# Attention before two expert layers on Trainium2: small products of 8 values a token, and of two inverse scales, made by POOL instead of VectorE

## The chip, the cores and the metric

The kernel runs on one core of one Trainium2 chip. A core has five engines, each of which runs its own instructions in order: TensorE (PE: matmuls, and transposes made by matmul), VectorE (DVE), ScalarE (ACT), GpSimd (POOL) and SyncE (SP, here the issuer of most DMAs). Engines wait for one another by semaphores. The metric is the time of one execution in microseconds on the device.

## The reference, cut to what matters

```
kv  = einsum('bhsd,bhse->bhde', k, v)             # 8 batches, 8 heads, 576 x 64
out = einsum('bhsd,bhde->bhse', q, kv)
out = out / sqrt(mean(out*out, -1) + 1e-6) * g_norm   # per token and head
x   = out as 4608 tokens x 512
h   = x @ w_in                                    # 512 x 2048
g   = max(h, 0) + alpha * min(h, 0)
y   = g @ w_out                                   # 2048 x 512
logits = y @ w_gate; e = argmax(logits)           # 8 experts, one per token
out = softmax(logits)[e] * sigmoid(y @ w_output_gate)[e] * (max(y @ w1[e], 0) @ w2[e])
```

For each token the norm needs 8 values, one per head: the sum of squares over 64 elements, its mean plus 1e-6, and that to the power -0.5. These 128x8 tiles (128 tokens, 8 heads) are what the change is about.

## The kernel before, in words

**Tiling.** 4608 tokens are 36 tiles of 128; three tiles make a block (12 blocks, i = 0 to 11). Products in 32 bits are made of three f16 matmuls: each operand is scaled by a power of two and split into a high and a low half ("hi", "lo"). For the scaling, pow2 (lines 108 to 121, three VectorE operations) turns a maximum into a scale and its inverse.

**Attention for block i** is att_steps(i), a list of steps that is fed between other work. For each tile, tr scales and splits q: qam is the maximum per head (line 273, VectorE), pow2 gives qsc and its inverse qiv, qiv is multiplied by the inverse scale kvi of kv (line 278 on 128 rows; for the ninth tile of a pair of batches line 282 does it on two halves of 64 rows), qs = q * qsc is made by POOL (line 284), split by ScalarE (287) and VectorE (288), and transposed by a DMA (290). Then om: matmuls into ops (line 311), ScalarE squares ops into xs (316), VectorE reduces xs to st, 128x8 (318), multiplies st twice by qiv (321), makes ms (323), and POOL raises ms to -0.5 into rs (325). Beside it VectorE takes the maximum of st over the heads, qm (328), and makes the power-of-two scale xinv of it (329 to 337). rs is multiplied by qm and qiv (340), ops by rs into xs (343); ScalarE and POOL split xs into x (347, 348), and a DMA transposes x into the block's tile (351). Blocks 0 and 1 take another way for q ("split_q" is false there), with no products by qiv.

**The first expert layer for block i.** 16 pieces h (h_piece, line 586, 12 matmuls each, two PSUM buffers): ScalarE makes m (589), VectorE r (591), ScalarE the hi half of g (593), VectorE its lo half (594; POOL in blocks 0 and 1). m and r have two buffers each. Then y (605), its maximum (655), the split into row (663 on ScalarE, 664 on VectorE), a DMA transpose to yT (668) and the logits l (678).

**Routing.** From the logits come the one-hot oh (up to 704), the rank matmuls rk (712 to 716), the positions pos (718 to 725), and three scatters by POOL (728), indirect DMAs that write the tokens' numbers into one list; each waits until the one before has landed. The rows are stored by SP (757, after 751).

**Order.** The program's text gives the steps in an order of interleaving, and a scheduler with a simulated timeline then sets the order on each engine, PE, ACT, DVE, POOL and SP alike; so a few changed instructions move others around them. In the last block and the second expert layer the order is set by hand.

Of the kernel before, what the change touches and what calls it, by code (L numbers as in the profile page):

```python
# [9 lines left out]
F32 = mybir.dt.float32  # L10
# [4 lines left out]
ALU = mybir.AluOpType  # L15
# [4 lines left out]
P = 128  # L20
B, H, S, D = 8, 8, 576, 64
# [29 lines left out]
EPS = 1e-6  # L51
# [6 lines left out]
def body(ctx: ExitStack, tc, q, k, v, g_norm, w_in, w_out, alpha, w_gate, w_og, w1, w2, out):  # L58
    nc = tc.nc
    pe, dve, act, pool, sp = nc.tensor, nc.vector, nc.scalar, nc.gpsimd, nc.sync  # L60
# [45 lines left out]
    def pow2(am, nm, out_s, out_inv, top=14, wide=False):  # L106


        e = small.tile([P, am.shape[1]], I32, tag="pw_e", name="pw_e" + nm, padded_shape=[P, E])
        dve.tensor_scalar(out=e, in0=am.bitcast(I32), scalar1=0x7FF00000 if wide else 0x7F800000, scalar2=None,  # L110
                          op0=ALU.bitwise_and)
        if wide:
            dve.tensor_scalar(out=e, in0=e, scalar1=float((896 + top + 1) << 20), scalar2=float((896 + 254) << 20),
                              op0=ALU.max, op1=ALU.min)
            dve.tensor_scalar(out=out_inv.bitcast(I32), in0=e, scalar1=8.0, scalar2=float(-((896 + top) << 23)),
                              op0=ALU.mult, op1=ALU.add)
        else:
            dve.tensor_scalar(out=out_inv.bitcast(I32), in0=e, scalar1=float((top + 1) << 23),
                              scalar2=float(-(top << 23)), op0=ALU.max, op1=ALU.add)
        dve.tensor_scalar(out=out_s.bitcast(I32), in0=out_inv.bitcast(I32), scalar1=-1.0, scalar2=float(254 << 23),  # L120
                          op0=ALU.mult, op1=ALU.add)
# [47 lines left out]
    kvp, qp, at = right("kvp", 2), right("qp", 2), right("at", 2)  # L169
# [74 lines left out]
    kv16, kvi = {}, {}  # L244
# [16 lines left out]
    def att_steps(i):  # L261
        G, t0 = divmod(i * TB, 9)
        ts = [t0 + u for u in range(TB)]
        qT, qi_ = {}, {}
        split_q = i >= SPLIT_Q

        def tr(t):
            nm = f"_{G}_{t}"
            n = 5 * G + t // 2
            qv = q_in[n][:, :, t % 2 if t < 8 else 0, :]  # L270
            if split_q:
                am = small.tile([P, H], F32, tag="am8", name="qam" + nm)
                dve.tensor_reduce(out=am, in_=qv, axis=AX.X, op=ALU.max, apply_absolute_value=True)
                s_ = small.tile([P, H], F32, tag="qsc", name="qsc" + nm)
                iv = qi_[t] = small.tile([P, H], F32, tag="qiv", name="qiv" + nm, bufs=4)
                pow2(am, "q" + nm, s_, iv)
                if t < 8:
                    dve.tensor_tensor(out=iv, in0=iv, in1=kvi[2 * G + t // 4], op=ALU.mult)
                else:
                    for half in range(2):  # L280
                        sl = slice(64 * half, 64 * half + 64)
                        dve.tensor_tensor(out=iv[sl], in0=iv[sl], in1=kvi[2 * G + half][sl], op=ALU.mult)
                qs = at.tile([P, H, D], F32, tag="xs", name="qs" + nm, bufs=3)
                pool.tensor_tensor(out=qs, in0=qv, in1=s_.unsqueeze(2).to_broadcast([P, H, D]), op=ALU.mult)
                qs = qs.rearrange("p a b -> p (a b)")
                q16 = at.tile([P, 2, DM], F16, tag="x16", name="q16" + nm)
                act.copy(out=q16[:, 0, :], in_=qs)
                dve.tensor_tensor(out=q16[:, 1, :], in0=qs, in1=q16[:, 0, :], op=ALU.subtract)
                qT[t] = at.tile([P, 2 * NC, P], F16, tag="qT", name="qT" + nm)
                sp.dma_start_transpose(out=qT[t], in_=q16.rearrange("p a b -> p (a b)"))  # L290
            else:
                qj = scratch[(1, 2, 0, 3, 4, 5)[t]]
                act.copy(out=qj.rearrange("p (h d) -> p h d", h=H), in_=qv)
                qps = ps_a.tile([P, NPAIR, P], F32, tag="a", name="qps" + nm)
                for hp in range(NPAIR):
                    pe.transpose(qps[:, hp, :], qj[:, hp * P:(hp + 1) * P], ident)
                qT[t] = at.tile([P, NPAIR, P], F32, tag="qT", name="qT" + nm)
                act.copy(out=qT[t], in_=qps)
            if t % 2 == 1 or t == 8:
                load_q(n + 2)  # L300

        def om(t):
            nm = f"_{G}_{t}"
# [11 lines left out]
            xs = at.tile([P, DM], F32, tag="xs", name="xs" + nm, bufs=3)  # L315
            act.activation(out=xs, in_=ops.rearrange("p a b -> p (a b)"), func=AF.Square)
            st = small.tile([P, H], F32, tag="st", name="st" + nm)
            dve.tensor_reduce(out=st, in_=xs.rearrange("p (h d) -> p h d", h=H), axis=AX.X, op=ALU.add)
            if split_q:
                for _ in range(2):  # L320
                    dve.tensor_tensor(out=st, in0=st, in1=qi_[t], op=ALU.mult)
            ms = small.tile([P, H], F32, tag="ms", name="ms" + nm)
            dve.tensor_scalar(out=ms, in0=st, scalar1=1.0 / D, scalar2=EPS, op0=ALU.mult, op1=ALU.add)
            rs = small.tile([P, H], F32, tag="rs", name="rs" + nm)
            pool.tensor_tensor(out=rs, in0=ms, in1=mhalf, op=ALU.pow)  # L325

# [880 lines left out]
```

## Time and profile before

| | us |
|---|---|
| median of 3 runs | 1522.31 |
| the 3 runs | 1513.83, 1522.31, 1522.7 |
| profiled execution, its own time | 1527.29 |
| its span, first to last instruction | 1525.5 |
| busy: PE | 1338.3 (88%) |
| busy: VectorE | 870.1 (57%) |
| busy: ScalarE | 580.7 (38%) |
| busy: POOL | 397.7 (26%) |

The profile is of one execution. Busy shares are means over the span, and the stages have different limits: to about 222 us weights and kv are prepared, 222 to 288 us is the end of the second block, then follow the steady blocks, and past some 1000 us the experts of the second layer, where VectorE and POOL have little to do. The time in front of an instruction in which its engine was idle is printed in brackets with what ended it. PEclk is TensorE's granted clock, in shares of full speed.

### The profile page before, as it was taken

The numbers are of one execution on the slowest core, as the hardware profiler recorded it, in microseconds if no ns is written. First come the engines' busy times: TensorE is split into PE (matmuls) and PEld (weight loads), VectorE is DVE, ScalarE is ACT, GpSimd is POOL, SyncE is SP. The second block draws the span as 40 slices with busy tenths as digits, with TensorE's granted clock in tenths as the row PEclk, the third lists the DMA queues.
The fourth block names the chain that finished last, engine by engine and source line by source line (L and its number), as shares of the span: only waits on it lengthen the run. The fifth ranks groups of instructions, "written<-read, shape, count | busy, mean of one in ns | idle before, by whom it ended". The sixth has DMA issues, their size and how long they took to land.

```text
span 1525.5 us, 22316 instructions
## 1 busy us (share of the span) xinstructions
PE 1338.3 (88%) x7586; PEld 680.4 (45%) x7586; DVE 870.1 (57%) x2406; ACT 580.7 (38%) x959; POOL 397.7 (26%) x383
## 2 busy tenths in 40 slices
PE   4687775698899898999999999998789978998998
PEld 3443332354445454555554555543333433443443
DVE  6888788675779696969696877535112112121221
ACT  3455535344556454655454655411111111111111
POOL 3455545232122232212121212011311111221211
PEclk9689888899999999999999999999899999999999
DMA  9732116646677677766745765147886986679665
GB/s 273 189 94 86 61 50 150 127 77 172 174 193 190 186 181 162 213 175 160 206 109 136 183 159 134 22 146 137 229 262 146 216 244 161 131 184 237 119 151 152
DMA packets 344835, 243.25 MB, mean 159 GB/s; under 512 B 267388, under 2 KB 300172, under 8 KB 342160
## 3 DMA queue, kind: packets, MB, share of 16 engines
q1 hardware_dynamic: 327792, 206.11, 55.3%
q0 software_dynamic: 7712, 18.92, 4.1%
q10 hardware_dynamic: 9216, 16.78, 3.3%
q8 instruction: 60, 0.98, 0.3%
q14 instruction: 55, 0.45, 0.1%
HBM read 244.66 MB, written 53.97 MB: 196 GB/s over the span
## 4 chain that ended last, share of the span: by engine, by line
PE 26%; DVE 19%; DMA 17%; issue 16%; SPq 14%; ACT 4%; POOL 3%; POOLq 0%; ACTq 0%; DVEq 0%
PE h L586 10%; PE y L605 6%; SPq L986 4%; PE bh_d L977 4%; PE bo_d L998 3%; DMA rawe<-in_moe_w_dram 3%; DMA yT<-row 3%; SPq L864 2%; DVE r L591 2%; SPq L949 2%; DMA out_dram<-ob_d,idx_d 2%; DMA hT_d<-h_d 2%; DMA ws<-wlo_w 2%; DVE wlo_w L387 1%; SPq L952 1%
## 5 line engine op out<-in xcount | busy, mean ns | idle before, releaser
L586 PE MATMUL h<-x,wi 128*128 128x384 f16 x2304 | 416.8, 333 | 28.0 <-ACT m L589 19.6
L605 PE MATMUL y<-wo,g 128*128 128x512 f16 x1728 | 416.4, 389 | 27.8 <-ACT wo L455 6.7
L586 PEld LDWEIGHTS <-wi 128*128 128x128 f16 x2304 | 224.4, 100 | 188.5 <-issue 38.5
L605 PEld LDWEIGHTS <-g 128*128 128x128 f16 x1728 | 167.4, 100 | 221.7 <-issue 40.6
L983 DVE CAST h_d<-br_d 128x512 f16<-128x512 f32 x74 | 32.3, 436 | 355.8 <-DMA hT_d<-h_d 314.1
L998 PE MATMUL bo_d<-lane,hT_d 128*128 128x512 f16 x888 | 206.3, 391 | 26.5 <-DMA hT_d<-h_d 26.5
L977 PE MATMUL bh_d<-lane,byT_d 128*128 128x512 f16 x888 | 202.2, 385 | 15.9 <-DMA byT_d<-yg 8.3
L998 PEld LDWEIGHTS <-hT_d 128*128 128x128 f16 x888 | 88.6, 100 | 139.3 <-DMA hT_d<-h_d 28.9
L593 ACT CAST g<-r 128x384 f16<-128x384 f32 x192 | 97.4, 509 | 133.4 <-DVE r L591 131.2
L591 DVE SCALAR_TENSOR_TENSOR r<-m,alphat 128x384 f32<-128x384 f32 x192 | 126.9, 662 | 30.1 <-ACT m L589 28.7
L977 PEld LDWEIGHTS <-byT_d 128*128 128x128 f16 x888 | 87.8, 99 | 124.6 <-DMA byT_d<-yg 8.8
L981 ACT ACTIVATE br_d<-bh_d 128x512 f32<-128x512 f32 x74 | 44.2, 597 | 208.3 <-PE bh_d L977 113.7
L325 POOL TENSOR_TENSOR rs<-ms,mhalf 128x8 f32<-128x8 f32 x36 | 67.0, 1864 | 173.9 <-DVE qm L328 158.3
L728 POOL DMA_INDIRECT lst<-ids,pos x36 | 39.2, 1090 | 271.4 <-DMA lst<-ids,pos 108.7
L594 DVE TENSOR_TENSOR g<-r,g 128x384 f16<-128x384 f32 x160 | 92.5, 579 | 24.2 <-ACT g L593 23.5
L589 ACT ACTIVATE m<-h,scal 128x384 f32<-128x384 f32 x160 | 91.5, 574 | 37.8 <-PE h L586 36.5
L387 DVE SCALAR_TENSOR_TENSOR wlo_w<-rawe,es_w,whi_w 128x1024 f16<-128x1024 f32 x64 | 87.1, 1376 | 27.1 <-ACT whi_w L386 10.7
L386 ACT ACTIVATE whi_w<-rawe,es_w 128x1024 f16<-128x1024 f32 x64 | 71.2, 1142 | 56.8 <-DMA ws<-whi_w 35.6
L856 POOL DMA_INDIRECT yg<-ytab,idx_d x37 | 38.2, 1032 | 188.1 <-issue 125.3
L1001 ACT ACTIVATE ob_d<-bo_d,msc_d 128x512 f32<-128x512 f32 x37 | 25.4, 687 | 162.3 <-PE bo_d L998 157.7
L526 ACT ACTIVATE eab_w<-rawe 128x1024 bf16<-128x1024 f32 x64 | 66.9, 1055 | 47.7 <-DMA rawe<-in_moe_w_dram 43.2
L1002 POOL DMA_INDIRECT out_dram<-ob_d,idx_d x37 | 39.0, 1055 | 165.4 <-ACT ob_d L1001 143.0
(304 smaller groups left out, 1395.8 us busy)
## 6 DMA issues: line engine op xcount, KB each, us to landing
lane<-ws SPq DMA_DIRECT2D x74, 2048.0 KB
rawe<-in_moe_w_dram SPq DMA_DIRECT2D x64, 512.0 KB
ws<-whi_w ACTq DMA_DIRECT2D x64, 256.0 KB
ws<-wlo_w SPq DMA_DIRECT2D x64, 256.0 KB
ytab<-row SPq DMA_DIRECT2D x32, 256.5 KB
q<-in_q_dram SPq DMA_DIRECT2D x16, 512.0 KB
rawwi<-in_moe_w_in_dram SPq DMA_DIRECT2D x16, 512.0 KB
rawwo<-in_moe_w_out_dram SPq DMA_DIRECT2D x16, 512.0 KB
```

Source lines behind the costliest of these rows:

```text
L325: pool.tensor_tensor(out=rs, in0=ms, in1=mhalf, op=ALU.pow)
L386: act.activation(out=dst_h, in_=src, func=AF.Copy, scale=s)
L387: dve.scalar_tensor_tensor(out=dst_l, in0=src, scalar=s, in1=dst_h, op0=ALU.mult, op1=ALU.subtract)
L526: act.activation(out=ab.rearrange("p a b -> p (a b)"), in_=raws[4 * m + i], func=AF.Abs)
L586: pe.matmul(ps, wi[:, f // 4 * NC + c, w, fs], xt[i][:, xc, :], start=(n == 0), stop=(n == 3 * NC - 1))
L589: act.activation(out=r0, in_=ps, func=AF.Copy, scale=(scst if start else scal)[:, f:f + 1])
L591: dve.scalar_tensor_tensor(out=r, in0=r0, scalar=alphat[:, f:f + 1], in1=r0, op0=ALU.mult, op1=ALU.max)
L593: act.copy(out=hi, in_=r)
L594: (pool if start else dve).tensor_tensor(out=lo, in0=r, in1=hi, op=ALU.subtract)
L605: pe.matmul(ps, g[:, t, f % GF, us], wo[:, f, w, :], start=(start and m == 0), stop=(stop and m == 2))
L977: pe.matmul(hp, j["yT"][:, x, :], w1_[:, w, c, hs], start=(m == 0), stop=(m == 3 * NC - 1))
L998: pe.matmul(po, hT[:, g, :], w2_[:, w, f, :], start=(m == 0), stop=(m == 3 * NFE - 1))
```

## The change

In blocks 2 to 11 (30 of 36 tiles) POOL makes what VectorE made: the two products of st by qiv and ms, 90 instructions, and the products of qiv by kvi, 26 on 128 rows and 8 on 64. The product qs on POOL is now issued before these. The power on POOL then follows ms on the same engine, while qm, on VectorE, reads an st that POOL writes. All 124 instructions keep their sizes.

```diff
--- before.py
+++ after.py
@@ -274,14 +274,14 @@
                 s_ = small.tile([P, H], F32, tag="qsc", name="qsc" + nm)
                 iv = qi_[t] = small.tile([P, H], F32, tag="qiv", name="qiv" + nm, bufs=4)
                 pow2(am, "q" + nm, s_, iv)
+                qs = at.tile([P, H, D], F32, tag="xs", name="qs" + nm, bufs=3)
+                pool.tensor_tensor(out=qs, in0=qv, in1=s_.unsqueeze(2).to_broadcast([P, H, D]), op=ALU.mult)
                 if t < 8:
-                    dve.tensor_tensor(out=iv, in0=iv, in1=kvi[2 * G + t // 4], op=ALU.mult)
+                    pool.tensor_tensor(out=iv, in0=iv, in1=kvi[2 * G + t // 4], op=ALU.mult)
                 else:
                     for half in range(2):
                         sl = slice(64 * half, 64 * half + 64)
-                        dve.tensor_tensor(out=iv[sl], in0=iv[sl], in1=kvi[2 * G + half][sl], op=ALU.mult)
-                qs = at.tile([P, H, D], F32, tag="xs", name="qs" + nm, bufs=3)
-                pool.tensor_tensor(out=qs, in0=qv, in1=s_.unsqueeze(2).to_broadcast([P, H, D]), op=ALU.mult)
+                        pool.tensor_tensor(out=iv[sl], in0=iv[sl], in1=kvi[2 * G + half][sl], op=ALU.mult)
                 qs = qs.rearrange("p a b -> p (a b)")
                 q16 = at.tile([P, 2, DM], F16, tag="x16", name="q16" + nm)
                 act.copy(out=q16[:, 0, :], in_=qs)
@@ -318,9 +318,9 @@
             dve.tensor_reduce(out=st, in_=xs.rearrange("p (h d) -> p h d", h=H), axis=AX.X, op=ALU.add)
             if split_q:
                 for _ in range(2):
-                    dve.tensor_tensor(out=st, in0=st, in1=qi_[t], op=ALU.mult)
+                    pool.tensor_tensor(out=st, in0=st, in1=qi_[t], op=ALU.mult)
             ms = small.tile([P, H], F32, tag="ms", name="ms" + nm)
-            dve.tensor_scalar(out=ms, in0=st, scalar1=1.0 / D, scalar2=EPS, op0=ALU.mult, op1=ALU.add)
+            (pool if split_q else dve).tensor_scalar(out=ms, in0=st, scalar1=1.0 / D, scalar2=EPS, op0=ALU.mult, op1=ALU.add)
             rs = small.tile([P, H], F32, tag="rs", name="rs" + nm)
             pool.tensor_tensor(out=rs, in0=ms, in1=mhalf, op=ALU.pow)
```

In the changed program the lines 278 and 280 are qs and qiv, and 284 the halves of qiv; all other lines keep their numbers. The scheduler's order differs from about 230 us on, at three engines as follows around the third block's first pieces h_0 to h_3 (block 2). The last number in a name tells tiles apart; st_0_2920 is the st of the first tile after the entry, m_0, r_0 and g belong to h_0, and pos_2616 and lst to the scatters of an earlier block, whose logits have just been made.

ScalarE there, before:

```order
L663 ACTIVATE row_0_2688<-g_179,sr_0_2681 128x512
L663 ACTIVATE row_1_2832<-g_179,sr_1_2825 128x512
L663 ACTIVATE row_2_2971<-g_179,sr_2_2964 128x512
L589 ACTIVATE m_0_2673<-h_0_2660,scal 128x384
L593 CAST g_176<-r_0_2675 128x384
L589 ACTIVATE m_1_2736<-h_1_2723,scal 128x384
L593 CAST g_176<-r_1_2738 128x384
```

and after:

```order
L589 ACTIVATE m_0_2673<-h_0_2660,scal 128x384
L663 ACTIVATE row_0_2688<-g_179,sr_0_2681 128x512
L663 ACTIVATE row_1_2832<-g_179,sr_1_2825 128x512
L593 CAST g_176<-r_0_2675 128x384
L663 ACTIVATE row_2_2971<-g_179,sr_2_2964 128x512
L589 ACTIVATE m_1_2736<-h_1_2723,scal 128x384
L593 CAST g_176<-r_1_2738 128x384
L589 ACTIVATE m_2_2770<-h_2_2757,scal 128x384
```

m_0 stood behind the three rows and stands ahead of them now; m_1 still stands behind the third row.

VectorE there, before:

```order
L591 SCALAR_TENSOR_TENSOR r_3_2819<-m_3_2817,alphat 128x384
L318 TENSOR_REDUCE st_0_2920<-xs_0_2918 128x8
L594 TENSOR_TENSOR g_176<-r_3_2819,g_176 128x384
L321 TENSOR_TENSOR st_0_2920<-st_0_2920,qiv_0_2696 128x8 x2
L679 TENSOR_REDUCE lg_521<-l_1_2895 128x16
L323 TENSOR_SCALAR ms_0_2924<-st_0_2920 128x8
L328 TENSOR_REDUCE qm_0_2928<-st_0_2920 128x1
L591 SCALAR_TENSOR_TENSOR r_4_2872<-m_4_2870,alphat 128x384
```

and after, where, on PE, rk stands behind the first 19 matmuls of h instead of ahead of them:

```order
L664 SCALAR_TENSOR_TENSOR row_2_2971<-g_179,sr_2_2964,row_2_2971 128x512
L723 TENSOR_REDUCE pf_2614<-rkk_2610 128x3
L591 SCALAR_TENSOR_TENSOR r_1_2738<-m_1_2736,alphat 128x384
L725 CAST pos_2616<-pf_2614 128x3
L594 TENSOR_TENSOR g_176<-r_1_2738,g_176 128x384
L591 SCALAR_TENSOR_TENSOR r_2_2772<-m_2_2770,alphat 128x384
L318 TENSOR_REDUCE st_0_2920<-xs_0_2918 128x8
L679 TENSOR_REDUCE lg_521<-l_0_2776 128x16
L594 TENSOR_TENSOR g_176<-r_2_2772,g_176 128x384
L328 TENSOR_REDUCE qm_0_2928<-st_0_2920 128x1
L591 SCALAR_TENSOR_TENSOR r_3_2819<-m_3_2817,alphat 128x384
```

pos_2616 stood ahead of all rows and pieces of this block, and stands behind r_1 now; st_0's products and ms are gone, and qm_0 stands between r_2 and r_3, where it was between r_3 and r_4.

POOL there, before:

```order
L348 TENSOR_TENSOR x_0_8_2498<-xs_8_2479,x_0_8_2498 128x512
L728 DMA lst<-ids,pos_2616 49152x1 x3
L284 TENSOR_TENSOR qs_2_2985<-q_2_2301,qsc_2_2978 128x512
L325 TENSOR_TENSOR rs_0_2926<-ms_0_2924,mhalf 128x8
L348 TENSOR_TENSOR x_1_0_2938<-xs_0_2918,x_1_0_2938 128x512
L325 TENSOR_TENSOR rs_1_3122<-ms_1_3120,mhalf 128x8
```

and after:

```order
L278 TENSOR_TENSOR qs_1_2794<-q_0_2191,qsc_1_2788 128x512
L280 TENSOR_TENSOR qiv_1_2789<-qiv_1_2789,kvi_2404 128x8
L280 TENSOR_TENSOR qiv_2_2979<-qiv_2_2979,kvi_2404 128x8
L728 DMA lst<-ids,pos_2616 49152x1
L278 TENSOR_TENSOR qs_2_2984<-q_2_2301,qsc_2_2978 128x512
L728 DMA lst<-ids,pos_2616 49152x1
L321 TENSOR_TENSOR st_0_2920<-st_0_2920,qiv_0_2696 128x8 x2
L323 TENSOR_SCALAR ms_0_2924<-st_0_2920 128x8
L325 TENSOR_TENSOR rs_0_2926<-ms_0_2924,mhalf 128x8
L728 DMA lst<-ids,pos_2616 49152x1
L348 TENSOR_TENSOR x_1_0_2938<-xs_0_2918,x_1_0_2938 128x512
```

The three scatters stood together; now st_0's products, ms and the power stand behind the second, and the third behind the power.

## Rows read from the trace of the kernel before

**Rows 1.** Table by stretches: length, busy us (instructions) of each engine, PEclk granted, DMA.

```profile
222.00:288.00 66.00, 40.23 (x304) 20.82 (x303) 55.55 (x186) 29.18 (x49) 30.82 (x26) 0.86 0.54 130
288.00:340.00 52.00, 48.51 (x339) 28.24 (x339) 37.10 (x116) 24.11 (x46) 14.48 (x11) 0.94 0.56 95
700.00:800.00 100.00, 98.15 (x649) 53.54 (x648) 80.50 (x230) 55.80 (x89) 23.41 (x18) 1.00 0.61 167
```

**Rows 2.** Waits of PE, 300 to 1000 us: waited for, us, times, longest.

```profile
PE l L678 <- DMA yT<-row: 9.1, 5, 3.5
...
PE h L586 <- ACT m L589: 6.5, 8, 2.0
```

**Rows 3.** Groups of instructions by line, VectorE.

```profile
L321 DVE TENSOR_TENSOR st<-st,qiv 128x8 f32<-128x8 f32 x60 | 9.6, 160 | 0.3
...
L278 DVE TENSOR_TENSOR qiv<-qiv,kvi 128x8 f32<-128x8 f32 x26 | 8.1, 326 | 0.1
...
L282 DVE TENSOR_TENSOR qiv<-qiv,kvi 64x8 f32<-64x8 f32 x8 | 3.0, 374 | 0.1
...
L323 DVE TENSOR_SCALAR ms<-st 128x8 f32<-128x8 f32 x36 | 6.5, 181 | 0.1
```

**Rows 4.** Timeline, VectorE: start, us, engine, line, operation.

```profile
257.82 0.15 DVE L323 TENSOR_SCALAR ms<-st 128x8 f32<-128x8 f32 x1
257.89 0.14 DVE L328 TENSOR_REDUCE qm<-st 128x1 f32<-128x8 f32 x1
```

**Rows 5.** Groups of instructions by line and shape, POOL.

```profile
L325 POOL TENSOR_TENSOR rs<-ms,mhalf 128x8 f32<-128x8 f32 x36 | 67.0, 1864 | 173.9 <-DVE qm L328 158.3 <-ACT m L589 7.0 <-DMA yT<-row 5.2
...
L284 POOL TENSOR_TENSOR qs<-q,qsc 128x512 f32<-128x512 f32 x30 | 35.8, 1203 | 52.3 <-DVE qm L328 22.4 <-issue 17.5 <-DVE qsc L120 10.2
...
L866 POOL TENSOR_TENSOR msc_d<-yg,kslot 128x1 f32<-128x1 f32 x37 | 8.0, 215 | 14.8 <-DMA yg<-ytab,idx_d 14.0
...
L104 POOL MEMSET mhalf<- 128x8 f32 x1 | 0.1, 104 | 0.1
```

**Rows 6.** Timeline, POOL and VectorE.

```profile
237.20 0.91 POOL L594 TENSOR_TENSOR g<-r,g 128x384 f16<-128x384 f32 x1
...
237.24 0.88 DVE L278 TENSOR_TENSOR qiv<-qiv,kvi 128x8 f32<-128x8 f32 x1
```

**Rows 7.** Timeline, PE, third block's entry.

```profile
286.68 0.20 PE L712 MATMUL rk<-oh,tri 128*128 128x24 f16 x1 [3.67 <-DVE oh L704]
...
288.38 6.75 PE L586 MATMUL h<-x,wi 128*128 128x384 f16 x24 [1.37 <-DMA x<-x]
...
298.28 1.95 PE L586 MATMUL h<-x,wi 128*128 128x384 f16 x11 [2.54 <-ACT m L589]
...
308.96 2.11 PE L586 MATMUL h<-x,wi 128*128 128x384 f16 x12
```

**Rows 8.** Timeline, POOL, the scatters there.

```profile
288.24 1.20 POOL L728 DMA_INDIRECT lst<-ids,pos  x1 [3.43 <-DVE row L751]
295.95 0.97 POOL L728 DMA_INDIRECT lst<-ids,pos  x1 [6.51 <-DMA lst<-ids,pos]
```

**Rows 9.** Timeline, ScalarE and VectorE, the same place.

```profile
297.04 0.72 ACT L663 ACTIVATE row<-g,sr 128x512 f16<-128x512 f32 x1 [1.05 <-DMA ytab<-row]
...
302.55 0.51 ACT L593 CAST g<-r 128x384 f16<-128x384 f32 x1 [0.77 <-DVE r L591]
...
302.97 0.57 ACT L589 ACTIVATE m<-h,scal 128x384 f32<-128x384 f32 x1
...
303.57 0.62 DVE L591 SCALAR_TENSOR_TENSOR r<-m,alphat 128x384 f32<-128x384 f32 x1
```

**Rows 10.** Timeline, VectorE and PE, two later places.

```profile
826.25 0.23 DVE L340 SCALAR_TENSOR_TENSOR rs<-rs,qm,qiv 128x8 f32<-128x8 f32 x1 [6.83 <-POOL rs L325]
...
827.75 0.38 PE L133 MATMUL allmax_w<-amdiag_w,ones 1*128 1x1 f32 x2 [1.24 <-DVE amdiag_w L132]
...
899.18 0.23 DVE L340 SCALAR_TENSOR_TENSOR rs<-rs,qm,qiv 128x8 f32<-128x8 f32 x1 [5.98 <-POOL rs L325]
```

## The prediction

> **What bounds the kernel now.** I looked first at the table by stretches, to see where TensorE (PE) is short of work. From 288 us on PE is busy 48.5 of 52 us, and in a late hundred 98.2 of 100; VectorE (DVE) in that hundred 80.5; POOL 23.4 [rows 1]. So in the blocks PE sets the pace, and VectorE, whose work the change takes, has a fifth of the time to spare. The one stretch that turns this round is 222 to 288 us: VectorE 55.6 of 66 us, PE 40.2 [rows 1]. There a shorter VectorE queue could be seen in the end.
>
> Second, the waits of PE between 300 and 1000 us. The logits wait 9.1 us for a transposed row, and the first products (h) 6.5 us in all for ScalarE's m [rows 2], which comes through VectorE's r. That 6.5 us is about all that a faster VectorE could give back in the steady blocks.
>
> Third, the timelines around the scatters (line 728). POOL runs its instructions in order; a scatter waits until the one before has landed, so that from the start of the first at 288.24 to that of the second at 295.95 there are 7.71 us, 6.51 of them idle [rows 8]. Whatever stands behind the second scatter in POOL's queue waits that long. This decides what the moved products cost, since in VectorE's queue nothing stood behind a scatter.
>
> **The change part by part.**
> *What VectorE loses.* 60 products st (160 ns), 30 of the 36 sums ms (181 ns), 26 products qiv on 128 rows (326 ns) and 8 on 64 rows (374 ns) [rows 3]: 9.6 + 5.4 + 8.5 + 3.0 = 26.5 us of summed durations. The queue gets less: two small operations that follow one another begin 0.07 us apart (257.82 and 257.89), each some 0.15 us long [rows 4]. So a removed one is worth 0.07 to 0.16 us, 124 of them 9 to 20 us, 0.3 to 0.7 us a tile. Cover: VectorE's own spare time beside PE. If the cover were gone, at most those 20 us would come back.
>
> *The lock.* The qiv products cost twice their like in st: the one at 237.24 ran 0.88 us and ended at 238.12, when POOL's g of 237.20 + 0.91 ended [rows 6]. On POOL the products stand in one queue with such work. The gain is 26 x 0.17 + 8 x 0.21 = 6 us of VectorE time, under the same cover.
> The Trainium skill (SBUF — State Buffer, the section on the two sides) says that a VectorE operation with two SBUF inputs and a GpSimd operation share one port pair as an exclusive lock, held for a whole instruction; the 0.88 us row agrees. By that rule the hold is not removed, but turned: POOL's small products would wait for VectorE's r, and r for them; that is the third rival.
>
> *What POOL gets.* 124 operations on 8 values. No row shows POOL multiplying 128x8. Nearest below: a fill of 128x8, 104 ns. Nearest in kind: a product on 128x1, 215 ns. Above: the power on 128x8, 1864 ns, and a product on 128x512, 1203 ns [rows 5]. I take 0.22 us, by the row of the same operation on small data, which is 124 x 0.22 = 27 us more on an engine busy a quarter of the time. By the ends it is 13 and 231 us; at the upper end the power would come 5.6 us late with its three in each tile, far beyond the cover.
>
> *The new wait.* qm (line 328) stays on VectorE but now needs st from POOL. Where VectorE made the two products itself in 0.16 us each [rows 3], it now waits for a handover and two products, some 0.5 us, and behind qm in its queue stand r and g of the next pieces of h. 30 x 0.5 = 15 us of VectorE queue: it eats the 9 to 20 us gained. Both lie under PE, so I set these two terms at 0, with 3 us to either side (half of the 6.5 us in rows 2).
>
> *Block 2's entry, where order changes most.* Before, PE did rk at 286.68 and h from 288.38, then stood 2.54 us before 298.28 for m [rows 7]. In the changed order 19 matmuls of h stand ahead of rk, and ScalarE's first m ahead of the three rows (line 663), which wait for stores. So pos comes late: VectorE's pos now stands behind r_1, this behind m_1, this behind the third row on ScalarE. That row began at 297.04 and took 0.72 [rows 9]; I take it as unmoved, since it waits for stores that the order leaves in place. Then m_1 begins near 297.8, r_1 ends near 299.0, and the first scatter starts at 299.1, not 288.24. The second follows 7.71 us later [rows 8], at 306.8, and ends near 307.8. The order on POOL puts st_0's two products right behind the second scatter; they end near 308.3. VectorE will reach qm_0 near 302 (r_2, st_0 and g_2 done) and stand there some 6.3 us, where before nothing held it. Behind it is r_3, begun at 303.57 before [rows 9], now at 308.4: 4.8 us late. PE has a lead: two h buffers and two of m, so it can do h_3 to h_5 meanwhile. h_6 needs m_4, behind g_3, behind r_3: 308.4 + 0.62 for r, 0.51 for g and 0.57 for m [rows 9] and the handovers give 310.2, where before h_6 began at 308.96 [rows 7]. **Cost +1.2 us**; bounds -3 (the rows come early too, the 2.54 us of wait falls away) and +7 (no lead, the whole hold).
>
> *Two later places.* Near 820 and 893 us the power already stood behind three scatters: VectorE was held 6.83 us until 826.25 and 5.98 us until 899.18, and PE stood 1.24 us before 827.75 for the small product behind the first of them [rows 10]. Now both products and the sum stand behind the scatters too. Three operations at 0.22 us and a handover come between the third scatter and the power: 0.7 to 1 us later each. Here the cover was used up before, so **+2 us**; bounds 0 and +6.
>
> *Where the cover holds.* At other scatters the products come after all three in the queue, as the power did; the wait is not new. Past 1000 us no step is moved: 0.
>
> Sum: +1.2 + 2 + 0 = **+3.2 us**. The profiled execution took 1527.29 us, 1525.5 of it span; the median of the three runs is 1522.31, 5 us below. So 1527.3 becomes 1530.5, and against the median I say **1525 us**. 1% is 15 us, about what a measurement can tell from no change.
>
> **The rivals.**
> *Relief that carries (faster, chance 0.13).* VectorE's 9 to 20 us and the 6 us of holds reach PE where VectorE is the chain: block 2 starts up to 3 us earlier, its 2.54 us wait goes, half of the 6.5 us on m goes, and of the reordered rest some 5 us. 3 + 2.5 + 3 + 5 = 13 us less, 1509. For it: 222 to 288 us with VectorE at 84%. Against: only that stretch has it, and PE's idle time after 300 us has mostly other causes, DMA first [rows 2].
>
> *POOL's queue becomes the bound (slower, chance 0.14).* st is ready before the second or third scatter of a block is issued, so the products wait for a landing and VectorE stands at qm with r and g behind it. It decides from the point where the hold is longer than PE's lead of about two pieces (some 5 us). Block 2 would cost its bound of 7, the two later places 3 each, and the 25 other tiles 0.2 each, 5: 18 us, 1540. For it: 6.5 us gaps, and the order at block 2. Against: elsewhere the scatters were there before the power too.
>
> *The lock turned round (chance 0.1).* Each of POOL's three small operations a tile waits for a running VectorE operation of 0.6 us (r took 0.62 at 303.57), and VectorE for POOL: 1.8 us more before qm, at three places uncovered, and a little elsewhere: +8 us, 1530.
> The rule of the Trainium skill (Perfetto Trace Analysis, the section on Scalar and DVE operations) is of this kind: moving work between these two might not help, because of the port they share.
>
> *All covered (0.1).* Neither handover nor scatter reaches PE, which is still at 98%: 1522.
>
> The forecast itself has 0.53. **Range 1508 to 1540**: the low end is the relief, the high end the blocked queue, and the half of each that lies beyond is what is left out, with a little for what I have not thought of. Faster by over 1% (below 1507): half of the relief and 0.04 of the unforeseen, 0.11. Slower by over 1% (above 1537.5): two thirds of the blocked queue and 0.05, 0.14. Within 1% 0.75.
>
> **What would show it.** Right: POOL's products at 128x8 near 0.22 us; VectorE busy some 20 us less; idle before line 328 of 10 to 20 us, released by POOL, the longest of 6 to 7 us ending near 308 us; the first scatter near 299 us; h_6 of block 2 near 310; near 828 us PE's wait for the small product near 2 us. Wrong: products of 1 us or more; waits of PE on m well above 6.5 us between 300 and 1000 us; a hold at line 328 in every block as long as a landing; or a block 2 that starts its h over 3 us earlier and keeps the lead to 1000 us.

## The result and the profile after

| | before | after |
|---|---|---|
| median of 11 runs, us | 1515.43 | 1533.67 |
| lowest to highest, us | 1508.78 to 1522.7 | 1519.1 to 1538.59 |
| ratio after to before | | 1.0107, 95% interval 1.0077 to 1.0137 |
| profiled execution: own time, span, us | 1527.29, 1525.5 | 1531.92, 1530.2 |

The change makes the kernel about 1.1% slower: 16 us by the ratio of all executions, 18 by the two medians, whose own ratio is 1.0120. Forecast were +3 us and a range that holds the new time. The ratios here and below leave out executions over 1.5% above the fastest of the same kernel, which are one of st only and one of first on POOL. The two profiles differ by 4.7 us only. That is because the execution whose profile stands ahead of the prediction took 12 us more than the median of its own kernel, while the one of after is near its median. The size of the change is therefore read from the medians, and the places from the traces.

The groups of POOL's instructions after the change, as [rows 5] show them before: shape, count, busy us, mean ns, and idle time ahead with what ended it.

```profile
L321 POOL TENSOR_TENSOR st<-st,qiv 128x8 f32<-128x8 f32 x60 | 24.5, 408 | 124.9 <-DVE st L318 86.3 <-DVE pw_eq L110 21.5 <-DVE sr L120 12.5
...
L280 POOL TENSOR_TENSOR qiv<-qiv,kvi 128x8 f32<-128x8 f32 x26 | 15.7, 605 | 1.4 <-DVE d L691 1.0 <-DVE qsc L120 0.3
...
L323 POOL TENSOR_SCALAR ms<-st 128x8 f32<-128x8 f32 x30 | 7.8, 259 | 2.7
...
L325 POOL TENSOR_TENSOR rs<-ms,mhalf 128x8 f32<-128x8 f32 x36 | 67.0, 1861 | 4.1 <-DVE qm L328 1.6
```

A product on 128x8 took 408 ns in the mean (its median was 297 and its shortest 199), the qiv products 605, ms 259. I had taken 220 for all. Of the 22 products and sums on 128x8 that took over 600 ns, 17 ended 57 to 67 ns after an instruction of VectorE had ended.

VectorE's qm and rs, the same columns, before:

```profile
L328 DVE TENSOR_REDUCE qm<-st 128x1 f32<-128x8 f32 x36 | 5.4, 151 | 0.0
...
L340 DVE SCALAR_TENSOR_TENSOR rs<-rs,qm,qiv 128x8 f32<-128x8 f32 x30 | 8.3, 278 | 14.9 <-POOL rs L325 14.8
```

and after:

```profile
L328 DVE TENSOR_REDUCE qm<-st 128x1 f32<-128x8 f32 x36 | 5.5, 154 | 21.8 <-POOL st L321 21.4
...
L340 DVE SCALAR_TENSOR_TENSOR rs<-rs,qm,qiv 128x8 f32<-128x8 f32 x30 | 8.9, 297 | 1.7 <-POOL rs L325 1.7
```

Before, nothing held qm, and rs (line 340) was held 14.9 us in all. Now qm is held 21.8 us, 21.4 of it by POOL, and rs 1.7: VectorE stops one step earlier.

The entry of the third block on PE, which answers to [rows 7] (start, duration, operation, in brackets the idle time ahead):

```profile
280.36 5.69 PE L586 MATMUL h<-x,wi 128*128 128x384 f16 x19 [3.20 <-DMA x<-x]
...
285.88 0.18 PE L712 MATMUL rk<-oh,tri 128*128 128x24 f16 x1
...
293.70 1.12 PE L586 MATMUL h<-x,wi 128*128 128x384 f16 x3 [3.82 <-ACT m L589]
...
306.29 3.54 PE L586 MATMUL h<-x,wi 128*128 128x384 f16 x12 [2.57 <-ACT m L589]
...
310.52 2.11 PE L586 MATMUL h<-x,wi 128*128 128x384 f16 x12
```

h starts at 280.36, 8 us earlier than the 288.38 of before, and its 19 matmuls come ahead of rk, as the order said. But PE then waits 3.82 us for m at 293.70, and 2.57 more at 306.29, where before it waited 2.54 us for m once, at 298.28 [rows 7].

ScalarE's third row, then POOL and VectorE there, which answer to [rows 8, 9]:

```profile
292.46 0.72 ACT L663 ACTIVATE row<-g,sr 128x512 f16<-128x512 f32 x1
...
295.32 1.22 POOL L728 DMA_INDIRECT lst<-ids,pos  x1 [15.07 <-DVE pos L725]
...
302.95 1.01 POOL L728 DMA_INDIRECT lst<-ids,pos  x1 [5.33 <-DMA lst<-ids,pos]
...
303.99 0.50 POOL L321 TENSOR_TENSOR st<-st,qiv 128x8 f32<-128x8 f32 x2
...
304.52 0.16 DVE L328 TENSOR_REDUCE qm<-st 128x1 f32<-128x8 f32 x1 [5.31 <-POOL st L321]
```

From the start of the first scatter to that of the second are 7.63 us (7.71 before). st_0's products run right behind it, and VectorE stands 5.31 us at qm. The forecast was this very hold, of 6.3 us, ending at 308.3; all of it came 4 us earlier. The forecast had built its times on a third row at 297.04, and that row came at 292.46.

The two later places, VectorE and PE, which answer to [rows 10]:

```profile
830.19 0.16 DVE L328 TENSOR_REDUCE qm<-st 128x1 f32<-128x8 f32 x1 [8.36 <-POOL st L321]
...
833.78 0.58 PE L133 MATMUL allmax_w<-amdiag_w,ones 1*128 1x1 f32 x2 [4.75 <-DVE amdiag_w L132]
...
905.26 0.16 DVE L328 TENSOR_REDUCE qm<-st 128x1 f32<-128x8 f32 x1 [6.67 <-POOL st L321]
...
906.43 0.27 PE L128 MATMUL allmax_w<-ident,amx_w 128*1 128x128 f32 x1 [2.70 <-DVE qm L329]
```

VectorE was held 8.36 and 6.67 us, PE 4.75 and 2.70 us behind it, where it had been 1.24 at the first.

What a PE wait leaves behind: the table by stretches (length, busy us of PE, PEld, DVE, ACT, POOL, PEclk granted, DMA share, GB/s).

```profile
306.20:309.80 3.60, 3.51 (x13) 1.57 (x12) 2.62 (x8) 2.13 (x5) 0.59 (x2) 0.58 0.00 0
...
310.50:312.60 2.10, 2.10 (x23) 1.32 (x20) 1.52 (x3) 0.99 (x2) 1.70 (x2) 1.00 0.01 0
...
833.70:837.00 3.30, 3.22 (x9) 1.53 (x10) 1.68 (x12) 1.75 (x3) 2.28 (x3) 0.50 0.19 38
```

After the 2.57 us of idle time the granted clock is 0.58 in the stretch of the next piece of h, whose 12 matmuls took 3.54 us; at 1.00, from 310.52 on, 12 matmuls took 2.11. After the 4.75 us it is 0.50. The levels are 1.2 and 2.4 GHz. So in this execution a wait of 2.6 us cost some 4 us of PE's time (2.57, and 3.54 against 2.11); my sum had no term for the clock.

PE's waits from 300 to 1000 us, as in [rows 2], after and then one line of before:

```profile
PE ops L311 <- DMA qT<-q: 13.7, 6, 5.1
...
PE h L586 <- ACT m L589: 5.5, 6, 2.6
...
PE allmax_w L133 <- DVE amdiag_w L132: 4.7, 1, 4.7
```

```profile
PE ops L311 <- DMA qT<-q: 7.8, 4, 5.0
```

The waits for m have not grown (5.5, 6.5 before; this stretch leaves out the 3.82 us at 293.70 and, before, the 2.54 at 298.28). The one at the later place is the 4.75 us seen above, and the waits for the transposed q are 13.7 us, where they were 7.8 in the first profile of before.

### The profile page after: what moved, and what is told of

It is laid out like the page before. It is cut to its first block, busy times and chain, and to the rows that moved or that the text cites. A ratio compares the mean times of both kernels' runs of the same rounds, so it can differ in the third digit from the quotient of the medians.

```text
span 1530.2 us, 22297 instructions
## 1 busy us (share of the span) xinstructions
PE 1348.8 (88%) x7586; PEld 684.6 (45%) x7586; DVE 862.7 (56%) x2282; ACT 581.8 (38%) x959; POOL 450.6 (29%) x507
## 4 chain that ended last, share of the span: by engine, by line
PE 38%; DMA 16%; issue 15%; DVE 15%; SPq 8%; POOL 4%; ACT 4%; POOLq 0%; DVEq 0%; ACTq 0%
PE h L586 12%; PE y L605 9%; PE bh_d L977 7%; PE bo_d L998 6%; SPq L986 2%; DVE r L591 2%; DMA hT_d<-h_d 2%; DMA rawe<-in_moe_w_dram 2%; DMA out_dram<-ob_d,idx_d 2%; DMA qT<-q 2%; SPq L864 2%; DMA ws<-wlo_w 2%; DMA yT<-row 1%; SPq L949 1%; POOL lst L728 1%
## 5 line engine op out<-in xcount | busy, mean ns | idle before, releaser
L586 PE MATMUL h<-x,wi 128*128 128x384 f16 x2304 | 422.3, 337 | 28.7 <-ACT m L589 18.9
L591 DVE SCALAR_TENSOR_TENSOR r<-m,alphat 128x384 f32<-128x384 f32 x192 | 130.6, 681 | 31.0 <-ACT m L589 30.0
L387 DVE SCALAR_TENSOR_TENSOR wlo_w<-rawe,es_w,whi_w 128x1024 f16<-128x1024 f32 x64 | 86.3, 1365 | 48.3 <-DMA ws<-wlo_w 21.8
L1002 POOL DMA_INDIRECT out_dram<-ob_d,idx_d x37 | 38.8, 1047 | 153.6 <-ACT ob_d L1001 132.7
L348 POOL TENSOR_TENSOR x<-xs,x 128x512 f16<-128x512 f32 x30 | 45.4, 1513 | 107.8 <-ACT x L347 105.2
```

Of the source, the lines that this page charges most:

```text
L387: dve.scalar_tensor_tensor(out=dst_l, in0=src, scalar=s, in1=dst_h, op0=ALU.mult, op1=ALU.subtract)
L586: pe.matmul(ps, wi[:, f // 4 * NC + c, w, fs], xt[i][:, xc, :], start=(n == 0), stop=(n == 3 * NC - 1))
L591: dve.scalar_tensor_tensor(out=r, in0=r0, scalar=alphat[:, f:f + 1], in1=r0, op0=ALU.mult, op1=ALU.max)
```

## The experiments

All ratios are to runs of the kernel before on the same chip; the experiments ran on four chips, so ratios are compared and not times. Three theories were on the table: **W**, qm waits for POOL's in-order queue, and VectorE with it; **L**, POOL's small products and VectorE hold each other by the shared port, wherever they stand; **O**, the new order as such, which the scheduler makes anew for every edit. W-scatter says that the holds behind scatters are what costs, W-spread that many short handovers are.

| run | edit | ratio | 95% interval |
|---|---|---|---|
| before again | none | 0.9966 | 0.9939 to 0.9993 |
| own products | VectorE makes its own st for qm | 1.0025 | 0.9996 to 1.0054 |
| st only | qiv stays on VectorE | 1.0127 | 1.0071 to 1.0183 |
| qiv only | st and ms stay on VectorE | 0.9972 | 0.9943 to 1.0001 |
| first on VectorE | the first tile of each block stays | 1.0013 | 0.9979 to 1.0047 |
| first on POOL | only the first tiles go | 1.0086 | 1.0054 to 1.0117 |
| one product | POOL makes the second product only | 0.9998 | 0.9968 to 1.0028 |
| qiv and ms | st's products stay | 1.0032 | 1.0000 to 1.0065 |
| change again | none | 1.0103 | 1.0064 to 1.0141 |
| POOL's product first | POOL makes the first product only | 1.0002 | 0.9971 to 1.0034 |
| entry on VectorE | one tile, near 300 us, stays | 1.0052 | 1.0030 to 1.0075 |
| late on VectorE | two tiles, near 825 and 900 us, stay | 1.0108 | 1.0075 to 1.0141 |

**Before again.** No edit.

> The kernel before once more, unchanged. It gives the size of a difference that means nothing, and a second profile: the first one's execution took 1527.29 us, 11.9 above the median of eleven runs, so part of what lies between the two profiles belongs to that execution. Every theory expects a ratio of 1.000, within 0.004. If the first profile was slow in its last part, past 1047 us, this one's span from the last rank matmul to the end is some 468 us instead of 478; if it was slow before that, the last rank matmul comes some 10 us before 1047.7.

The same program came out 0.34% faster, its interval just short of 1: differences of 0.3% say nothing here. Its profiled execution took 1505.09 us against 1527.29 for the other, and the last rank matmul came at 1029.42 instead of 1047.71 us; from there to the end it took 474.0 us instead of 477.8. So the slow part of the first profile lay mostly before 1047 us. PE's waits in this one, 300 to 1000 us:

```profile
PE ops L311 <- DMA qT<-q: 5.3, 5, 3.1
...
PE h L586 <- ACT m L589: 6.4, 8, 1.9
```

The wait for q is 5.3 us here and 7.8 in the first profile, that for m 6.4 and 6.5: part of what looks like a gain or a loss between two traces is the execution.

**Own products.**

```diff
 # ... (st0 is the st that VectorE reduced; st and stp are new tiles; ms reads stp)
+                for j in range(2):
+                    dve.tensor_tensor(out=st, in0=st if j else st0, in1=qi_[t], op=ALU.mult)
+                    pool.tensor_tensor(out=stp, in0=stp if j else st0, in1=qi_[t], op=ALU.mult)
-                    pool.tensor_tensor(out=st, in0=st, in1=qi_[t], op=ALU.mult)
```

> POOL makes the products of st, ms and those of qiv as in the change, in a tile of its own; VectorE makes the two products of st a second time, for qm alone. So POOL has all the work of the change and VectorE nothing less but ms and qiv, and qm waits for POOL nowhere. Theory W (qm waits for POOL, behind scatters above all, and VectorE stands with r and g behind it): ratio to before 0.998 to 1.004, no idle time before qm's line released by POOL, PE's wait for the small product near 830 us under 2 us. Rival L (POOL's small products hold VectorE and the other way round by the shared port, wherever they stand): as slow as the change or slower, 1.009 to 1.014, since both engines now do them.

1.0025: most of the cost is gone, though POOL does all that it does in the change. qm (now line 331, from VectorE's own tile sq) waits for nothing:

```profile
L331 DVE TENSOR_REDUCE qm<-sq 128x1 f32<-128x8 f32 x30 | 4.5, 152 | 0.1
```

So the products on POOL are not what costs, and theory L falls as the main cause. It doesn't part W from O: the scheduler's order is another here too, with the rows ahead of m_0 at the entry. The Trainium skill (SBUF — State Buffer, the section on the two sides) has the lock between these two engines; products in the changed kernel that took up to 1179 ns against a shortest of 199, and the 17 long ones that ended just behind an instruction of VectorE, agree with one, but here it does not set the time.

**st only** (the two products and ms to POOL) and **qiv only** (the other half of the change).

```diff
 # st only: line 321 as in the change, ms too; lines 278 to 284 as before
 # qiv only: lines 276 to 284 as in the change; st and ms as before (...)
-                    pool.tensor_tensor(out=st, in0=st, in1=qi_[t], op=ALU.mult)
+                    dve.tensor_tensor(out=st, in0=st, in1=qi_[t], op=ALU.mult)
```

> Only the two products of st and ms go to POOL; the products of qiv stay on VectorE where they were. Theory W: nearly all of the change's cost, 1.008 to 1.012, with idle time before qm's line near 20 us. Rival L: part of it by the count of operations, 90 of 124, 1.007. Rival O (the reordering alone, by chance): anything from 0.997 to 1.012.

> Only the products of qiv go to POOL, behind qs; st and ms stay on VectorE. Theory W: no qm waits for POOL, 0.998 to 1.003. Rival L: 34 of 124 operations, but the longer ones, 1.003 to 1.005. Rival O: as in the run with st alone, anything up to 1.012.

1.0127 and 0.9972: the whole cost goes with the products of st and ms, none with those of qiv, as W said. But O goes along with it: st only has m_0 ahead of the rows at the entry, qiv only has the rows ahead. The 34 operations of qiv are off VectorE without any gain that can be measured. **qiv and ms** takes ms with them:

```diff
 # qiv only, and
-            dve.tensor_scalar(out=ms, in0=st, scalar1=1.0 / D, scalar2=EPS, op0=ALU.mult, op1=ALU.add)
+            (pool if split_q else dve).tensor_scalar(out=ms, in0=st, ...)
```

> POOL makes the products of qiv and ms; both products of st stay on VectorE, so qm waits for nothing of POOL's. 64 operations leave VectorE and none of them makes it wait. Theory W: no cost, 0.995 to 1.001. Rival L: half of the cost, 1.004 to 1.006.

1.0032 lies between the two expectations and within the 0.34% by which the kernel before differs from itself: no verdict. Nothing held qm (0.1 us in all).

**First on VectorE** and **first on POOL.**

```diff
 # first on POOL has the condition turned round; ms has the same condition (...)
                 for _ in range(2):
-                    pool.tensor_tensor(out=st, in0=st, in1=qi_[t], op=ALU.mult)
+                    (dve if t == t0 else pool).tensor_tensor(out=st, in0=st, in1=qi_[t], op=ALU.mult)
```

> The change, but in the first tile of each block the two products of st and ms stay on VectorE; the other 20 of 30 tiles have them on POOL. In the order of POOL only first tiles have products behind a scatter. Theory W-scatter (the cost sits in the three holds of 5 to 8 us at qm behind scatters, and in the half clock after them): most of it goes, ratio to before 1.000 to 1.005, no idle time over 1 us before qm's line. Rival W-spread (20 and more short handovers, VectorE late in every tile): two thirds stay, 1.007 to 1.010. Rival L (the port): 64 + 34 of 124 operations stay, 1.008.

> The complement: only in the first tile of each block POOL makes the products of st and ms; in the other 20 VectorE does. qiv's products on POOL. Theory W-scatter: nearly the whole cost, 1.008 to 1.013, with three holds of 5 to 8 us at qm. Rival W-spread: a third, 1.002 to 1.005. Rival L: 1.004.

1.0013 with 20 tiles on POOL, 1.0086 with the other 10. qm's line in the first and then in the second:

```profile
L328 DVE TENSOR_REDUCE qm<-st 128x1 f32<-128x8 f32 x36 | 5.6, 155 | 1.7 <-POOL st L321 1.5
```

```profile
L328 DVE TENSOR_REDUCE qm<-st 128x1 f32<-128x8 f32 x36 | 5.5, 153 | 15.6 <-POOL st L321 15.5
```

Twenty handovers hold qm 1.7 us in all and cost nothing that stands clear of the noise; ten first tiles hold it 15.6 us, most of it in three holds of 3.9, 6.3 and 4.7 us, where 5 to 8 were expected. That speaks against W-spread.

**One product**, and later **POOL's product first.**

```diff
 # POOL's product first: (pool, dve)
-                for _ in range(2):
-                    pool.tensor_tensor(out=st, in0=st, in1=qi_[t], op=ALU.mult)
+                for e in (dve, pool):
+                    e.tensor_tensor(out=st, in0=st, in1=qi_[t], op=ALU.mult)
```

> The change, but VectorE makes the first of the two products of st and POOL only the second. qm waits for POOL as before, for 30 operations fewer. Theory W: the cost stays, 1.009 to 1.013, since it is the place in POOL's queue that costs and not the products; idle before qm's line near 20 us. Rival L: a quarter less by the count, 1.008 or less.

0.9998: a miss for W. L's "1.008 or less" was open below and so is not decided by it, though none of the cost that L gives to the products left on POOL is there. The three holds are there, but shorter than in the change (3.81, 5.16 and 1.25 us); VectorE at the entry and at the first later place:

```profile
295.26 0.16 DVE L328 TENSOR_REDUCE qm<-st 128x1 f32<-128x8 f32 x1 [3.81 <-POOL st L321]
...
819.25 0.16 DVE L328 TENSOR_REDUCE qm<-st 128x1 f32<-128x8 f32 x1 [5.16 <-POOL st L321]
```

> As the run with one product, which cost nothing, but with the two turned round: POOL makes the first product of st and VectorE the second. Count and engines are the same. What differs is VectorE's order at the place near 820 us: the instruction that now waits for POOL is VectorE's second product, and the weights' maximum (amx_w, which PE waits for) stands behind it, where in the run with one product it stood ahead of the waiting qm. Theory W-scatter with its refinement (a hold costs only where something that PE needs soon stands behind it): some of the cost is back, 1.004 to 1.011, with a wait of PE for that maximum of 2 us and more near 820 us. Rival C (the count of products on POOL decides): 0.997 to 1.003 as the run with one product.

1.0002: a second miss, for the refined theory. The trace shows what was expected there, and the time doesn't. VectorE's holds of 4.00 and 7.14 us, and PE's two waits for the weights' maximum:

```profile
295.26 0.17 DVE L321 TENSOR_TENSOR st<-st,qiv 128x8 f32<-128x8 f32 x1 [4.00 <-POOL st L321]
...
813.70 0.17 DVE L321 TENSOR_TENSOR st<-st,qiv 128x8 f32<-128x8 f32 x1 [7.14 <-POOL st L321]
...
814.66 0.27 PE L128 MATMUL allmax_w<-ident,amx_w 128*1 128x128 f32 x1 [3.03 <-DVE qm L329]
...
889.84 0.27 PE L128 MATMUL allmax_w<-ident,amx_w 128*1 128x128 f32 x1 [2.10 <-DVE qm L329]
```

So long holds at the two later places, with 5 us of PE waits behind them, cost nothing measurable, and I had to take W-scatter apart by place. The hold of 4.00 us at the entry, 3.81 in the run before, cost nothing measurable either: a hold behind a scatter is not enough. In both kernels the rows stand ahead of m_0 at the entry.

**Change again.**

> The changed kernel once more, for a second profile and a second interval. Ratio to before 1.0077 to 1.0137 as first measured. Theory W-scatter: the holds of 4 to 8 us at qm stand at the same three places, near 300, 830 and 905 us, and PE again waits 2 us and more behind the latter two for the small products of the weights' maximum; the half clock after them too. If the holds are an accident of one execution, they are elsewhere or half as long.

1.0103. VectorE's holds and PE's waits in this second execution:

```profile
305.79 0.16 DVE L328 TENSOR_REDUCE qm<-st 128x1 f32<-128x8 f32 x1 [4.73 <-POOL st L321]
...
824.51 0.16 DVE L328 TENSOR_REDUCE qm<-st 128x1 f32<-128x8 f32 x1 [8.30 <-POOL st L321]
...
295.55 0.72 PE L586 MATMUL h<-x,wi 128*128 128x384 f16 x3 [4.46 <-ACT m L589]
...
307.55 2.11 PE L586 MATMUL h<-x,wi 128*128 128x384 f16 x12 [2.89 <-ACT m L589]
...
828.10 0.38 PE L133 MATMUL allmax_w<-amdiag_w,ones 1*128 1x1 f32 x2 [4.69 <-DVE amdiag_w L132]
```

The holds are no accident: 5.31 and 4.73 us at the entry, 8.36 and 8.30 at the first later place, 6.67 and 4.05 at the second. PE's wait at the second, 2.70 us in the first execution, is a miss: here it didn't wait there at all. The two waits for m at the entry are there again too (3.82 and 2.57; 4.46 and 2.89). The clock behind them is not the same each time. By the table of stretches it was 1.00 after the 2.89 us here, and 0.57 after the 4.69:

```profile
307.50:311.00 3.50, 2.94 (x26) 1.84 (x26) 2.52 (x8) 2.03 (x4) 0.51 (x1) 1.00 0.00 0
...
828.00:831.50 3.50, 3.40 (x10) 1.46 (x11) 2.08 (x12) 1.95 (x3) 2.46 (x3) 0.57 0.24 47
```

So half clock at the entry is no constant part of the cost; in late on VectorE too it was 1.00 after a wait of 2.80 us.

**Entry on VectorE** and **late on VectorE.** They change one and two tiles of the 30, and leave the order of the change as it is ahead of them. Behind them the scheduler made another one: in the first kernel PE's order (by names without their numbers) differs from the change's at 989 of 7586 places, between 310 and 750 us, in the second at 323, past 825 us. The change itself differs from before at 1332.

```diff
 # late on VectorE: i > 9 and t == t0; ms has the same condition (...)
-                    pool.tensor_tensor(out=st, in0=st, in1=qi_[t], op=ALU.mult)
+                    (dve if i == 3 and t == t0 else pool).tensor_tensor(out=st, in0=st, in1=qi_[t], op=ALU.mult)
```

> The change, but in one tile, the first after the third block's entry (st_0 near 300 us), VectorE makes the two products of st and ms. The order of all engines is that of the change up to there, and qm_0 no longer waits behind the second scatter. Open after ten runs: which of the three holds costs the 1%, since the run with POOL's product first had holds of 4.0, 7.1 and 6.2 us and PE waits of 5 us behind the two later ones, and cost nothing measurable. Theory E (the entry: the h pieces that the hold stops, with the half clock behind it, and all that follows): 1.000 to 1.005. Theory A (the two late places, near 825 and 900 us): 1.008 to 1.012 as the change. If each place bears a share: 1.005 to 1.008.

> The complement: only in the two late tiles, near 825 and 900 us, VectorE makes the products and ms; the order of all engines is that of the change until some 810 us, the hold at the entry included. Theory E: 1.007 to 1.012. Theory A: 1.000 to 1.004. Shares: 1.004 to 1.007.

1.0108 without the two late ones: their products cost nothing. 1.0052 without the one at the entry: about half of the cost is gone with the three instructions moved back and the order that came with it. The two intervals just touch, and by the medians of these two kernels, 1537.68 and 1532.72 us, the difference is 5 us and not 8.5. In the first of the two kernels, PE at the entry, then VectorE's rs there:

```profile
296.98 1.12 PE L586 MATMUL h<-x,wi 128*128 128x384 f16 x3 [5.60 <-ACT m L589]
...
309.26 0.23 DVE L340 SCALAR_TENSOR_TENSOR rs<-rs,qm,qiv 128x8 f32<-128x8 f32 x1 [4.38 <-POOL rs L325]
```

The wait of 5.60 us for m at 296.98 is still there (it comes from the order, m_1 behind the third row), and rs is now held behind the second scatter instead of qm; but PE's second wait for m, 2.57 us in the change, is not among the waits above 1 us. The entry as a whole is no shorter: from the first rank matmul to the second it took 49.7 us here, 47.4 and 46.8 in the two executions of the change. What is gone is a wait for the transposed q, 140 us later. PE there in the change, then in this kernel:

```profile
446.20 1.46 PE L311 MATMUL ops<-kv,qT 128*128 128x128 f16 x12 [5.07 <-DMA qT<-q]
```

```profile
445.61 0.83 PE L311 MATMUL ops<-kv,qT 128*128 128x128 f16 x12
```

It was 3.88 us in change again and 5.16 in late on VectorE. So the gain may be the order's and not the hold's; nor does this one execution show where it lies, since PE's idle time from the second rank matmul to the eighth, 28.4 us, is about that of the change (30.4 and 28.0). In the second kernel the entry is as in the change, and at the later place rs is held as qm was:

```profile
304.86 0.16 DVE L328 TENSOR_REDUCE qm<-st 128x1 f32<-128x8 f32 x1 [5.35 <-POOL st L321]
...
306.62 2.11 PE L586 MATMUL h<-x,wi 128*128 128x384 f16 x12 [2.80 <-ACT m L589]
...
828.66 0.23 DVE L340 SCALAR_TENSOR_TENSOR rs<-rs,qm,qiv 128x8 f32<-128x8 f32 x1 [8.14 <-POOL rs L325]
...
829.85 0.38 PE L133 MATMUL allmax_w<-amdiag_w,ones 1*128 1x1 f32 x2 [3.08 <-DVE amdiag_w L132]
```

So there the hold only changes its name, and PE waits 3.08 us for the same small product, though VectorE makes st and ms there as before the change. PE's order is the change's until 825 us in this kernel, and its cost is the change's: what costs lies ahead of the two late places, or in the order behind them.

**What stays open.** Which part of the cost is the hold's and which the order's is not shown. In every kernel that cost over 0.5%, qm reads an st of which POOL makes both products in eight to ten of the ten first tiles; but each of these kernels has an order of its own too. The traces give a lead, no more. In the kernels whose scheduler put m_0 ahead of the rows at the entry (the change, st only, entry and late on VectorE), the stretch from the second rank matmul to the eighth, with no long hold at qm in the change, took 474.6 to 480.8 us; in the six that put the rows or xs_0 first and cost nothing clear of the noise, 462.5 to 475.4. PE was idle 28 to 30 us in it in the four kernels (five executions), and 19 to 26 in the six. In the change and in late on VectorE the wait for the transposed q makes 12 to 14 us of it, and 3 to 8 elsewhere. That speaks for theory O: another order on PE, in which ops stands where less other work covers its transfer. Against it: the kernel before, one and the same order, took 474.2 us in its first execution and 462.7 in its second, with PE idle 29.0 and 19.7 us, so that one program spans most of the difference; st only, the slowest kernel, has 6.6 us of the wait for q; and first on POOL cost 0.86% with the rows ahead of m_0, as before. These are single executions, and no kernel changed the order alone, or the hold alone.

## Why the prediction was right, and where its sum was not

- **Direction and size.** Slower, as said; but the sum was +3.2 us and the measured difference is 16 to 18, five times as much. That the new time lies in the range is in part luck: the range reached up to the blocked queue's 1540, and it was built on a median of three runs, 1522.31, that eleven runs put at 1515.43. By its ratio the change is slower by over 1%, which had a chance of 0.14.
- **The hold and its place.** VectorE stands at qm behind a scatter: right. At the entry it was 5.31 us (forecast 6.3), the first scatter at 295.32 (299.1), the second 7.63 later (7.71). All came 4 us early because I took the third row as unmoved at 297.04, and it came at 292.46. The second execution of the kernel before had it at 292.27, so that its time says little of the change.
- **The entry's price, +1.2 us.** I set h_6 against its time before, 310.2 against 308.96. It came at 306.29 and, in change again, at 307.55; in the second execution of before it came at 305.59. By that measure the entry gained up to 2.7 us or lost up to 2, which is the difference of two executions: no trace shows a price there. The run with the entry's tile on VectorE gave 1.0052 against 1.0108, 0.0056 x 1524 = 8.5 us, over my bound of +7, or 5 us by the medians; but as that run reordered PE as well, it doesn't price the hold. This term is not measured.
- **The two later places, +2 us.** PE's wait grew from 1.24 to 4.75 us at the first, more than said. But without their products the time is the same, 1.0108, so this term is 0: with the products on VectorE the power stands behind the same scatters, and PE waited 3.08 us there as well.
- **Price of a product, 0.22 us.** Measured 0.41 in the mean, within the bounds. It was covered: own products (1.0025) and first on VectorE (1.0013) cost nothing clear of the noise.
- **Handovers and relief, both 0.** Held: 20 tiles' handovers 1.7 us and 1.0013; qiv's 34 operations off VectorE 0.9972, where before again had 0.9966.
- **What the sum lacked.** It has no term for the reordered blocks past the entry: they were put at nothing, for the scatters there alone, and the order of PE, ScalarE and VectorE was not looked at. What was measured of the terms that it has doesn't make up the cost: the late places gave 0, and no trace shows a price at the entry. The mean stretch from the second rank matmul to the eighth is 477.7 us in the two executions of the change and 468.4 in the two of before, 9 us more, though each pair differs by 6 to 11 us in itself. That the order is the cause stays open.
- **The rivals.** The blocked queue was the nearest: its sign, and about its size (18 us, measured 16). The size is luck: its two later places and its 25 other tiles, 11 of the 18 us, cost nothing that could be measured. The lock turned round would have lengthened the products at the three holds. At all three the two products took 0.50 us together, so there it did not; away from qm it fell to the run with own products. Relief fell to qiv only.

No kernel here beats the one before beyond 0.3%, the difference of that kernel from itself.

## What to carry to other kernels

An operation that moves to an in-order engine takes over that engine's waits, and gives them to whoever reads its result: before moving a small product, list what stands ahead of it in the new queue, scatters above all. Here holds of 5 to 8 us went from rs to qm, or arose at qm. Whether they cost anything is another matter: two kernels with holds of up to 5 and 7 us cost nothing. The duration of the operation hardly mattered, 0.4 us each. Where a scheduler sets the order, an edit of three instructions put others at a thousand places of PE's order, so compare kernels in the same order before a cost is put down to the edit. And measure the same program twice before pricing a difference of a few us by two traces: here the two profiles said 5 us and the medians 18.

## What was not expected of the hardware

The same program had profiled executions of 1505.09 and 1527.29 us, 1.5% apart, 14.5 us of it between the first and the last rank matmul (761.0 and 746.5 us). A PE wait of 2.57 us was followed by a granted clock of 0.58, one of 2.89 us in another execution of the same program by 1.00. And POOL's product of 128x8 took from 199 to 1179 ns, the long ones mostly until just after an instruction of VectorE had ended.
